# z by DMA transpose and VectorE, tile 0's transposes together, another order of x and W1, and two tiles joined one k step earlier

## The chip, the cores and the metric

The kernel runs on one core of a Trainium2 chip. The metric is the device time of a run in microseconds (us); the median of several runs is given. A profiled run also gives the span, from the first to the last instruction, which is some 2 us shorter here than the run's time.

A core has five engines with an instruction queue each, which run in order and wait for each other by semaphores: TensorE (PE; its weight loads are listed as PEld), VectorE (DVE), ScalarE (ACT), GpSimd (POOL) and SyncE (SP), which only issues DMAs here. Matmuls write into PSUM, which has eight banks of 512 fp32 columns on 128 partitions.

## The reference

The input x has 2048 tokens of 640 features. It is normalized, and the result goes through a linear attention of 32 heads of 20 features and through a GELU MLP with 1536 hidden features. The three terms are added:

```python
xn = _layernorm(x, axis=-1)
return x + _A_ref(xn, A_wqkv, A_wo) + _B_ref(xn, B_w1, B_b1, B_w2, B_b2)

# _A_ref, for each head
phi = lambda t: jnp.where(t > 0, t + 1, jnp.exp(t)) + 1e-6
pq, pk = phi(q), phi(k)
kv = jnp.einsum("bhsd,bhse->bhde", pk, v)
z = jnp.einsum("bhsd->bhd", pk)              # sum of phi(k) over all tokens
num = jnp.einsum("bhqd,bhde->bhqe", pq, kv)
den = jnp.einsum("bhqd,bhd->bhq", pq, z)[..., None] + 1e-6
o = num / den                                # then o @ wo

# _B_ref
h = _gelu(x @ w1 + b1)
return h @ w2 + b2
```

So z holds one number for each of the 640 columns of phi(k): its sum over the 2048 tokens.

## The kernel before

Tokens lie in 16 tiles of 128 (NT = 16, P = 128, DT = 640 / 128 = 5, JT = 1536 / 128 = 12). A planner gives each instruction its waits from what it reads and writes. Within an engine the order is that of the program text.

The stages: (1) x and W1 are loaded, tiles are normalized on VectorE and transposed, and h = gelu(xn @ W1 + b1) is made, with W1's 128x128 blocks as weights and the transposed tokens as moving columns; (2) k and phi(k); (3) G = xn^T phi(k), from which k^T v follows later; (4) q and phi(q), with z and KVT in between; (5) the outputs.

**Loads.** All of these are issued by SyncE, in this order:

```python
for i, (lo, hi) in enumerate(((0, XA), (XA, D))):
    dma(("sync", s_)[i], x_in[:, 0, lo:hi], xv[0:P, lo:hi], [r_x[0][i]])   # second part: ScalarE
dma_x(1, 1)
dma_w1(0)
dma_w1(1)
dma_w1(2)
dma_x(2, 1)
dma_w1(3)
dma_x(3, 1)
dma_w1(4)
dma_x(4, 2)
dma_x(6, 2)
dma_x(8, 2)
dma_x(10, 2)
```

dma_x(t, n) loads tiles t to t+n-1 (160 KB each), dma_w1(k) rows 128k to 128k+127 of W1 (384 KB).

**Tiles 0 to 2** are transposed on TensorE, into banks 6 and 7, and copied from there; tiles 3 to 15 by a DMA transpose that SyncE issues (xnT_dma). PARTS says for a part of tile 0 or 1: bank, first and last 128-column block, copying engine.

```python
PARTS = [((6, 0, 1, s_), (7, 1, 3, s_), (6, 3, DT, s_)), ((6, 0, 3, s_), (7, 3, DT, v))]
# tr_part(t, i): the transposes of part i on TensorE (L342)
# cp_part(t, i): its copy to xnT by ScalarE (L350) or VectorE (L351)
...
tr_part(0, 0)
cp_part(0, 0)
b1_copy()
filler(2, P)
tr_part(0, 1)
cp_part(0, 1)
```

**h of tiles 0 and 1** is built up k step by k step, as W1's row blocks come in, in banks 0 to 5 (hk, L439): one matmul for a block of 128 hidden features, an n of 1 or 2 tiles (128 or 256 moving columns) and one k. Later tiles take whole k sums (h_pack L423, h_unit L408).

```python
plan = k_list(0, 1, [0]) + ["T1"] + k_list(0, 1, [1]) + k_list(1, 1, [0]) + k_list(1, 1, [1]) + ["TC"]
plan += k_list(0, 1, [2]) + k_list(1, 1, [2]) + k_list(0, 2, [3], 0, 8) + ["T2"]
plan += k_list(0, 2, [4], 0, 8) + k_list(0, 2, [3, 4], 8)
plan += pack(2, 0, 8) + h_list(2, 2, 8, JT) + pack(3, 0, 8) + h_list(4, 2, 0, 7) + h_list(6, 2, 0, 7)
plan += h_list(4, 4, 7, JT) + h_list(8, 4, 0, JT) + h_list(12, 4, 0, JT)

def ln_rest():
    def out(t):
        ln_norm(t)
        xnT_dma(t)
    ln_stats(5); out(4); ln_stats(6); out(5)
    ln_stats(7); out(6); out(7)
    dma_x(12, 4)
    ln_stats(8)
    ...                                   # tiles 8 to 15 in the same way

if u == "TC":
    tr_part(0, 2); cp_part(0, 2)
elif u == "T1":
    for i in range(2):
        tr_part(1, i); cp_part(1, i)
    ln_stats(2); ln_half(3, 0); ln_half(3, 1); ln_norm(2); ln_aggr(3)
elif u == "T2":
    at(7)
    b = transp(2)
    ln_norm(3); xnT_dma(3)
    xnT_copy(2, b)
    ln_stats(4); ln_rest()
```

ln_stats is the statistics of a tile (two halves and their aggregate), ln_norm its normalization, all on VectorE with a small step on GpSimd; transp and xnT_copy are tile 2's transposes and copy.

**z.** During stage 3 VectorE adds phi(k) of the 16 tiles (z_sums, L617 and L620), which leaves 128 partial sums for each of the 640 columns, and splits them into a bf16 value and a bf16 remainder (zhl, two times 640 columns, L623 and L626). z_step adds the 128 partitions by a matmul with a column of ones, and spreads z into ZB, the weights of the denominator's matmuls:

```python
def z_step():
    b = take(1)
    Pl.ins(pe, [(lambda e, j=j, i=i: e.matmul(bank(b, j, j + 1), zhl[:, i, j * P:(j + 1) * P], onesm[:, 0:1],
                                              start=(i == 0), stop=(i == 1)))       # L632
                for j in range(DT) for i in range(2)],
           reads=[r_zhl, r_ones], writes=[B_[b]])
    Pl.ins(v, lambda e: e.tensor_copy(z_sb[:], bank(b, 0, DT)), reads=[B_[b]], writes=[r_z])   # L636
    for j in range(DT):
        Pl.ins(v, lambda e, j=j: e.tensor_scalar(ZB[:, j, :], hmask[:, j // 2, :], z_sb[:, j:j + 1], None, ALU.mult),
               reads=[r_z, r_hmask], writes=[r_ZB])                                  # L638

z_sums()
for f in range(DT):
    g_group(f)          # stage 3, L597
g_rem()                 # L606; its result is transposed by DMA, as GrT
...
q_chunk(0)              # q of tiles 0-3: 5 x 5 matmuls L650, phi: ScalarE L552, VectorE L553 and L555
z_step()
kvt_step()              # L660; VectorE masks (L667)
q_chunk(1)
q_chunk(2)
q_chunk(3)
...
out_mm(0, 0, JT, MAIN, first[:1])   # 12 matmuls of output tile 0
den_mm(bb[1])                       # denominators: reads ZB and all of phi(q), head block by head block (L714)
m_step(...)                         # L704
```

The phi instructions on VectorE (0.29 us for L553 and 0.69 us for L555) are issued in each q_chunk, one pair for each of its five banks.

Of the kernel before, what the change touches and what calls it, by code (L numbers as in the profile page):

```python
# [5 lines left out]
ALU = AluOpType  # L6
ACT = mybir.ActivationFunctionType
P = 128
# [104 lines left out]
def bass_parallel_sum__linear_attn_block__dense_activation_gelu__prompt_kernel(  # L113
# [27 lines left out]
    with contextlib.ExitStack() as es:  # L141
# [23 lines left out]
        zsum = Mf[:, 0:2 * D].bitcast(FP32)  # L165
        PKT = Mf[:, 0:NC * CW]
        GrT = Mf[:, 4 * D:5 * D]
        zhl = Mf[:, 2 * D:4 * D].rearrange("p (a d) -> p a d", a=2)
        b1tmp = sb("b1tmp", [JT, P], BF16)
        b1c = sb("b1c", [P, JT], FP32)  # L170
# [8 lines left out]
        aggr = sb("aggr", [P, 4, 2], FP32)  # L179
        rstd = sb("rstd", [P, NT], FP32)  # L180
        mhalf = sb("mhalf", [P, 1], FP32)
        z_sb = sb("z_sb", [P, DT], FP32)
        ek = sb("ek", [P, 3, D], BF16)
        den_sb = sb("den_sb", [P, CW], FP32)
# [55 lines left out]
        r_KVP = [R_("KVP%d" % i) for i in range(3)]  # L240
        r_WqP = R_("WqP")
        r_M = [[R_("M%d_%d" % (j, h)) for h in range(2)] for j in range(DT)]
        r_zsum, r_zhl, r_z, r_ZB = R_("zsum"), R_("zhl"), R_("z"), R_("ZB")
        r_den, r_rden = R_("den"), R_("rden")
        r_rsp = [[R_("rsp%d_%d" % (c, r)) for r in range(3)] for c in range(NC)]
        r_out = [R_("out0"), R_("out1")]
# [18 lines left out]
        def dma_x(t, n):  # L265
            dma("sync", x_in[:, t:t + n, :], xv[t * P:(t + n) * P, :].rearrange("(t p) d -> p t d", p=P),
                sum(r_x[t:t + n], []))

        def dma_w1(k):
            dma("sync", W1[:, k, :], w1v[:, k, :], [r_W1[k]])  # L270
# [3 lines left out]
            dma(("sync", s_)[i], x_in[:, 0, lo:hi], xv[0:P, lo:hi], [r_x[0][i]])  # L274
        dma_x(1, 1)
        dma_w1(0)
        dma_w1(1)
        dma_w1(2)
        dma_x(2, 1)
        dma_w1(3)  # L280
        dma_x(3, 1)
        dma_w1(4)
        dma_x(4, 2)
        dma_x(6, 2)
        dma_x(8, 2)
        dma_x(10, 2)

        Pl.ins(v, lambda e: e.memset(pm[0:P // 2], 1.0), writes=[r_pm])
        Pl.ins(v, lambda e: e.memset(pm[P // 2:P], -1.0), writes=[r_pm])
# [41 lines left out]
        def b1_copy():  # L331
            Pl.ins(s_, lambda e: e.activation(b1c[:], b1T, ACT.Copy), reads=[B_[6]], writes=[r_b1c])

        PARTS = [((6, 0, 1, s_), (7, 1, 3, s_), (6, 3, DT, s_)), ((6, 0, 3, s_), (7, 3, DT, v))]

        def xT(t, k):
            return r_xnT[t][next(i for i, (_, lo, hi, _) in enumerate(PARTS[t]) if lo <= k < hi)]
# [1 line left out]
        def tr_part(t, i):  # L339
            b, lo, hi, _ = PARTS[t][i]  # L340
            pT = bank(b).bitcast(BF16)
            Pl.ins(pe, [(lambda e, k=k: e.transpose(  # L342
                pT[:, k * P:(k + 1) * P], xn_tm[:, t, k * P:(k + 1) * P], ident[:]))
                for k in range(lo, hi)], reads=[r_xn[t][min(i, len(r_xn[t]) - 1)], r_ident], writes=[B_[b]])

        def cp_part(t, i):
            b, lo, hi, eng = PARTS[t][i]
            tok = slice(t * P, (t + 1) * P)
            src = bank(b).bitcast(BF16)[:, lo * P:hi * P].rearrange("p (k q) -> p k q", q=P)
            Pl.ins(eng, lambda e: e.activation(xnT[:, lo:hi, tok], src, ACT.Copy) if eng == s_ else  # L350
                   e.tensor_copy(xnT[:, lo:hi, tok], src), reads=[B_[b]], writes=[r_xnT[t][i]])  # L351

        def ln_half(t, h):
            s = t % 4
            cut = XA if t == 0 else HW
            lo, hi = ((0, cut), (cut, D))[h]
            Pl.ins(v, lambda e: e.bn_stats(stats[:, s, 6 * h:6 * h + 6], x_in[:, t, lo:hi]),  # L357
                   reads=[r_x[t][min(h, len(r_x[t]) - 1)]], writes=[r_stats[s][h]])
            if h == 0:
                Pl.ins(g, lambda e: e.tensor_single_scalar(stats[:, s, 2:3], stats[:, s, 2:3], D * EPS, ALU.add),  # L360
                       reads=[r_stats[s][0]], writes=[r_stats[s][0]])
# [8 lines left out]
        def ln_stats(t):  # L370
            ln_half(t, 0)
            ln_half(t, 1)
            ln_aggr(t)

        def ln_norm(t, part=None):
            s = t % 4
            for i, r in enumerate(r_xn[t]):
                if part not in (None, i):
                    continue
                lo, hi = (0, D) if len(r_xn[t]) == 1 else ((0, P), (P, D))[i]  # L380
                Pl.ins(v, lambda e, lo=lo, hi=hi: e.tensor_scalar(
                    xn_tm[:, t, lo:hi], x_in[:, t, lo:hi], aggr[:, s, 0:1], rstd[:, t:t + 1],
                    ALU.subtract, ALU.mult),
                    reads=r_x[t] + [r_aggr[s], r_rstd[t]], writes=[r])
# [86 lines left out]
        b1_copy()  # L471
        filler(2, P)
        tr_part(0, 1)
        cp_part(0, 1)

        h_list = lambda t, n, lo, hi: [(t, n, jb) for jb in range(lo, hi)]
        k_list = lambda t, n, ks, lo=0, hi=JT: [(t, n, jb, ks) for jb in range(lo, hi)]
        pack = lambda t, lo, hi: [(t, jb) for jb in range(lo, hi, 4)]
        plan = k_list(0, 1, [0]) + ["T1"] + k_list(0, 1, [1]) + k_list(1, 1, [0]) + k_list(1, 1, [1]) + ["TC"]
        plan += k_list(0, 1, [2]) + k_list(1, 1, [2]) + k_list(0, 2, [3], 0, 8) + ["T2"]  # L480
        plan += k_list(0, 2, [4], 0, 8) + k_list(0, 2, [3, 4], 8)
        plan += pack(2, 0, 8) + h_list(2, 2, 8, JT) + pack(3, 0, 8) + h_list(4, 2, 0, 7) + h_list(6, 2, 0, 7)
        plan += h_list(4, 4, 7, JT) + h_list(8, 4, 0, JT) + h_list(12, 4, 0, JT)
# [1 line left out]
# [4 lines that stand above are left out]
            ln_stats(5)  # L489
            out(4)  # L490
            ln_stats(6)
            out(5)
            ln_stats(7)
            out(6)
            out(7)
            dma_x(12, 4)
            ln_stats(8)
            for t in range(8, NT):
                if t + 1 < NT:
                    ln_stats(t + 1)  # L500
                out(t)

        for u in plan:
            if u == "TC":
                tr_part(0, 2)
                cp_part(0, 2)
            elif u == "T1":
                for i in range(2):
                    tr_part(1, i)
                    cp_part(1, i)  # L510
                ln_stats(2)
                ln_half(3, 0)
                ln_half(3, 1)
                ln_norm(2)
                ln_aggr(3)
            elif u == "T2":
                at(7)
                b = transp(2)
                ln_norm(3)
                xnT_dma(3)  # L520
                xnT_copy(2, b)
                ln_stats(4)
                ln_rest()
            elif len(u) == 2:
                h_pack(*u)
            elif len(u) == 4:
                hk(*u)
            else:
                h_unit(*u)
# [98 lines left out]
                       reads=[r_zsum, r_zhl], writes=[r_zhl])  # L628

        def z_step():  # L630
            b = take(1)
            Pl.ins(pe, [(lambda e, j=j, i=i: e.matmul(bank(b, j, j + 1), zhl[:, i, j * P:(j + 1) * P], onesm[:, 0:1],  # L632
                                                      start=(i == 0), stop=(i == 1)))
                        for j in range(DT) for i in range(2)],
                   reads=[r_zhl, r_ones], writes=[B_[b]])
            Pl.ins(v, lambda e: e.tensor_copy(z_sb[:], bank(b, 0, DT)), reads=[B_[b]], writes=[r_z])  # L636
            for j in range(DT):
                Pl.ins(v, lambda e, j=j: e.tensor_scalar(ZB[:, j, :], hmask[:, j // 2, :], z_sb[:, j:j + 1], None, ALU.mult),  # L638
                       reads=[r_z, r_hmask], writes=[r_ZB])

        z_sums()
        for f in range(DT):
            g_group(f)
        g_rem()
# [103 lines left out]
                   reads=[r_xr[t // CH], r_b2], writes=[r_xb[t]])  # L748

        q_chunk(0)  # L750
        z_step()
        kvt_step()
        q_chunk(1)
        q_chunk(2)
# [139 lines left out]
```

## Time and profile before

| | before |
|---|---|
| time, median of 3 | 206.3 us (206.2 to 206.43) |
| span of the profiled run | 204.5 us |
| VectorE busy | 107.6 us (53%) |
| ScalarE busy | 70.6 us (35%) |
| DMA queue of SyncE and that of ScalarE | 32.7% and 6.4% of 16 DMA engines' span |
| moved by DMA | 21.37 MB, mean 105 GB/s |

A line of a timeline has its start and its length in us, the engine, the line of the kernel (L632), the operation, what it writes and reads, the shapes and how many instructions are merged in it; in square brackets stands how long the engine was idle before it, and what ended that. "SPq" is SyncE's queue: for it, the length is that of issuing, not of the transfer. A line of DMA issues ends with the median time from issue to landing. The chain of waits is followed back from the last instruction: at each step to what released it, or to the instruction before it on its engine.

### The profile page before, as it was taken

To read this page: it belongs to the slowest core of one execution; us is meant where nothing else is said; L and a number is where in the kernel's file an instruction comes from. 1 tells how busy PE (TensorE), PEld (TensorE's weight loads), DVE (VectorE), ACT (ScalarE), POOL (GpSimd) and SP (SyncE) were. 2 spreads that over 40 slices of the span, in tenths; PEclk is the share of its full clock that TensorE was granted. 3 is DMA by queue.
4 is the path that set the end of the run, shared out by engine and by line. 5 is a ranking of instruction groups with operands and counts; after the bars stand their busy time and mean duration, and the time that the engine had idled before them with its cause. 6 is when DMAs were issued, how large, how long until landed. Compare 5 with 4: busy or idle time off the path is not lost.

```text
span 204.5 us, 3338 instructions
## 1 busy us (share of the span) xinstructions
PE 201.2 (98%) x1230; PEld 104.0 (51%) x1230; DVE 107.6 (53%) x237; ACT 70.6 (35%) x138; POOL 34.1 (17%) x85
## 2 busy tenths in 40 slices
PE   8999999999999999999999999999999999999995
PEld 3899864444444444444546444544444444444443
DVE  3588764000007889499658888534624823513231
ACT  2369976666676555121163554500000000000000
POOL 3235637400000001898000200000000000000000
PEclk9999999999999999999999999999999999999999
DMA  5997678899700111100010000238985622102301
GB/s 161 368 277 93 136 162 99 233 332 363 250 6 0 26 26 26 29 0 0 0 32 5 0 0 16 92 51 197 321 206 127 152 54 55 51 26 51 79 29 51
DMA packets 34457, 21.37 MB, mean 105 GB/s; under 512 B 21384, under 2 KB 33800, under 8 KB 34440
## 3 DMA queue, kind: packets, MB, share of 16 engines
q1 hardware_dynamic: 30384, 17.54, 32.7%
q10 hardware_dynamic: 4056, 3.61, 6.4%
q8 instruction: 10, 0.16, 0.3%
q14 instruction: 7, 0.06, 0.1%
HBM read 13.08 MB, written 2.62 MB: 77 GB/s over the span
## 4 chain that ended last, share of the span: by engine, by line
PE 96%; DVE 1%; DMA 1%; issue 0%; DVEq 0%
PE ps L771 29%; PE ps L408 20%; PE ps L650 11%; PE ps L564 8%; PE ps L597 8%; PE ps L782 7%; PE ps L439 3%; PE ps L423 2%; PE ps L606 2%; PE ps L570 2%; DMA xPK<-in_A_x_dram 1%; DVE stats L357 1%; PE ps L704 1%; PE ps L660 1%; PE ps L714 1%; PE ps L342 0%
## 5 line engine op out<-in xcount | busy, mean ns | idle before, releaser
L771 PE MATMUL ps<-W,HG 128*128 128x512 bf16 (+2 forms) x204 | 43.9, 367 | 0.0
L408 PE MATMUL ps<-xnT,W 128*128 128x512 bf16 (+1 forms) x235 | 41.5, 338 | 0.0
L412 ACT ACTIVATE HG<-ps,b1c 128x512 bf16<-128x512 f32 (+1 forms) x47 | 27.9, 651 | 12.1 <-PE ps L408 11.6
L408 PEld LDWEIGHTS ps<-xnT,W 128*128 128x128 bf16 x235 | 22.8, 98 | 18.0
L771 PEld LDWEIGHTS ps<-W,HG 128*128 128x128 bf16 x204 | 19.4, 98 | 22.2 <-ACT Msb L686 0.2
L552 ACT ACTIVATE ek<-ps 128x512 bf16<-128x512 f32 x40 | 23.8, 597 | 19.4 <-PE ps L650 10.1
L553 DVE TENSOR_SCALAR ek<-ek 128x512 bf16<-128x512 bf16 x40 | 11.5, 287 | 31.4 <-ACT ek L552 31.4
L795 DVE TENSOR_TENSOR W<-ps,xnT 128x512 bf16<-128x512 f32 x15 | 10.4, 691 | 25.1 <-PE ps L771 19.4
L650 PE MATMUL ps<-xnT,Wqkv 128*128 128x512 bf16 x100 | 21.9, 379 | 0.0
L771 PE MATMUL ps<-Msb,PQ 128*128 128x512 bf16 (+2 forms) x85 | 19.6, 367 | 0.0
L564 PE MATMUL ps<-Wqkv,xnT 128*128 128x512 bf16 x80 | 17.9, 379 | 0.0
L591 POOL COPY Wqkv<-Wqkv 128x128 bf16<-128x128 bf16 x25 | 13.9, 558 | 22.4 <-PE ps L570 20.9
L597 PE MATMUL ps<-xPK,xn_tm 128*128 128x512 bf16 x80 | 17.4, 379 | 0.0
L357 DVE BATCH_NORM_STATS2 stats<-xPK 128x6 f32<-128x320 bf16 (+2 forms) x32 | 13.9, 478 | 5.7 <-DMA xPK<-in_A_x_dram 5.7
L650 PEld LDWEIGHTS ps<-xnT,Wqkv 128*128 128x128 bf16 x100 | 9.7, 98 | 11.5
L555 DVE SCALAR_TENSOR_TENSOR PQ<-ps,ek 128x512 bf16<-128x512 f32 x20 | 13.8, 692 | 2.5 <-PE ps L632 0.5
L771 PEld LDWEIGHTS ps<-Msb,PQ 128*128 128x128 bf16 x85 | 8.2, 98 | 9.2
L597 PEld LDWEIGHTS ps<-xPK,xn_tm 128*128 128x128 bf16 x80 | 7.8, 98 | 9.4
L564 PEld LDWEIGHTS ps<-Wqkv,xnT 128*128 128x128 bf16 x80 | 7.8, 98 | 9.4
L555 DVE SCALAR_TENSOR_TENSOR xPK<-ps,ek 128x512 bf16<-128x512 f32 x16 | 11.1, 692 | 1.7
L620 DVE TENSOR_TENSOR Msb<-Msb,xPK 128x640 f32<-128x640 f32 x14 | 11.6, 826 | 0.5
L367 POOL TENSOR_TENSOR rstd<-aggr,mhalf 128x1 f32<-128x1 f32 x16 | 10.0, 623 | 7.4 <-DVE aggr L365 7.4
(79 smaller groups left out, 151.1 us busy)
## 6 DMA issues: line engine op xcount, KB each, us to landing
Wqkv<-in_A_wqkv_dram SPq DMA_DIRECT2D x3, 800.0 KB, 7.4
xnT<-in_A_x_dram SPq DMA_DIRECT2D x4, 512.0 KB, 6.9
W<-in_B_w_dram SPq DMA_DIRECT2D x5, 384.0 KB, 5.2
W<-in_B_w_dram SPq DMA_DIRECT2D x1, 1920.0 KB, 13.1
out_dram<-W ACTq DMA_DIRECT2D x15, 128.0 KB, 1.8
xn_tm<-rden ACTq DMA_DIRECT2D x12, 128.0 KB, 4.6
xPK<-in_A_x_dram SPq DMA_DIRECT2D x4, 320.0 KB, 7.1
Wo<-in_A_wo_dram SPq DMA_DIRECT2D x8, 160.0 KB, 8.7
```

The source lines that it names most:

```text
L357: Pl.ins(v, lambda e: e.bn_stats(stats[:, s, 6 * h:6 * h + 6], x_in[:, t, lo:hi]), reads=[r_x[t][min(h, len(r_x[t]) - 1)]], writes=[r_stat ...
L408: Pl.ins(pe, [(lambda e, k=k: e.matmul(bank(b, 0, w), W1[:, k, jb * P:(jb + 1) * P], xnT[:, k, tok], start=(k == 0), stop=(k == DT - 1))) ...
L412: Pl.ins(s_, lambda e: e.activation(HG[:, jb, tok], bank(b, 0, w), ACT.Gelu_apprx_tanh, bias=b1c[:, jb:jb + 1]), reads=[B_[b], r_b1c], wri ...
L552: Pl.ins(s_, lambda e: e.activation(e2, src, ACT.Exp), reads=br, writes=[r_ek[s]])
L555: Pl.ins(v, lambda e: e.scalar_tensor_tensor(out=d2, in0=src, scalar=0.0, in1=e2, op0=ALU.max, op1=ALU.add), reads=br + [r_ek[s]], writes= ...
L564: Pl.ins(pe, [(lambda e, k=k, b=b, t=t: e.matmul(bank(b), xnT[:, k, t * P:(t + 1) * P], Wqkv[:, k, D:D + MW], start=(k == 0), stop=(k == D ...
L591: Pl.ins(g, lambda e, k=k, i=i: e.tensor_copy(plain(Wqkv[:, k, D:2 * D], i), parts(Wqkv[:, k, 0:D], i)), reads=[r_Wq], writes=[r_Wk, r_WqP])
L597: Pl.ins(pe, lambda e, t=t, b=b, f=f, i=i: e.matmul(bank(b), xn_tm[:, t, f * P:(f + 1) * P], PK[:, t, 0:MW], start=(i == 0), stop=(i == NT ...
L620: Pl.ins(v, lambda e, t=t: e.tensor_tensor(out=zsum, in0=zsum, in1=PK[:, t, :], op=ALU.add), reads=[r_PK[t], r_PKr[t // CH], r_zsum], writ ...
L650: Pl.ins(pe, [(lambda e, k=k, j=j, b=b: e.matmul(bank(b), Wqkv[:, k, D + j * P:D + (j + 1) * P], xnT[:, k, cc], start=(k == 0), stop=(k == ...
L771: Pl.ins(pe, [(lambda e, i=i, x=x, bk=bk: e.matmul(bank(bk, 0, x[1] - x[0]), seq[i][0], seq[i][1][:, x[0]:x[1]], start=(i == 0), stop=(i = ...
L782: Pl.ins(pe, lambda e, i=i: e.matmul(bank(b), seq[i][0], seq[i][1], start=(i == 0), stop=(i == NS - 1)), reads=seq[i][2], writes=[B_[b]], ...
```

## The change

The change has five parts.

1. z's sum over partitions leaves TensorE: the two times 640 columns of zhl are transposed by DMA (ten blocks of 128x128), VectorE adds along the row and adds value and remainder. This is issued right after z_sums, so it stands before q's phi in VectorE's order. The PSUM bank of the old step is no longer taken.
2. The third part of tile 0's transposes goes into bank 7 and is done right after the second.
3. Tiles 0 and 1 are joined (256 moving columns) from k step 2 on, by counting from 0, instead of from k step 3.
4. Loads: x2 and x3 come between W1's row blocks 0, 1 and 2; x8 to x11 are issued behind tile 5's DMA transpose.
5. Statistics, copies and normalizations of tiles 1 to 3 are reordered on VectorE, and tile 3's normalization and DMA transpose come before tile 2's transposes are used.

```diff
+        zT = Mf[:, 0:2 * D].rearrange("p (a q) -> p a q", q=P)
...
+        z2 = sb("z2", [P, 2 * DT], FP32)
...
         dma_x(1, 1)
         dma_w1(0)
+        dma_x(2, 1)
         dma_w1(1)
+        dma_x(3, 1)
         dma_w1(2)
-        dma_x(2, 1)
         dma_w1(3)
-        dma_x(3, 1)
         dma_w1(4)
         dma_x(4, 2)
         dma_x(6, 2)
-        dma_x(8, 2)
-        dma_x(10, 2)
...
-        PARTS = [((6, 0, 1, s_), (7, 1, 3, s_), (6, 3, DT, s_)), ((6, 0, 3, s_), (7, 3, DT, v))]
+        PARTS = [((6, 0, 1, s_), (7, 1, 3, s_), (7, 3, DT, s_)), ((6, 0, 3, s_), (7, 3, DT, v))]
...
         tr_part(0, 1)
+        tr_part(0, 2)
         cp_part(0, 1)
+        cp_part(0, 2)
...
-        plan = k_list(0, 1, [0]) + ["T1"] + k_list(0, 1, [1]) + k_list(1, 1, [0]) + k_list(1, 1, [1]) + ["TC"]
-        plan += k_list(0, 1, [2]) + k_list(1, 1, [2]) + k_list(0, 2, [3], 0, 8) + ["T2"]
+        plan = k_list(0, 1, [0]) + ["T1"] + k_list(0, 1, [1]) + k_list(1, 1, [0]) + k_list(1, 1, [1])
+        plan += k_list(0, 2, [2]) + k_list(0, 2, [3], 0, 8) + ["T2"]
...
             out(4)
             ln_stats(6)
             out(5)
+            dma_x(8, 2)
+            dma_x(10, 2)
             ln_stats(7)
...
-            if u == "TC":
-                tr_part(0, 2)
-                cp_part(0, 2)
-            elif u == "T1":
-                for i in range(2):
-                    tr_part(1, i)
-                    cp_part(1, i)
+            if u == "T1":
+                tr_part(1, 0)
+                cp_part(1, 0)
+                tr_part(1, 1)
                 ln_stats(2)
                 ln_half(3, 0)
+                cp_part(1, 1)
+                ln_norm(2)
                 ln_half(3, 1)
-                ln_norm(2)
                 ln_aggr(3)
+                ln_norm(3)
+                xnT_dma(3)
             elif u == "T2":
                 at(7)
                 b = transp(2)
-                ln_norm(3)
-                xnT_dma(3)
                 xnT_copy(2, b)
...
         def z_step():
-            b = take(1)
-            Pl.ins(pe, [(lambda e, j=j, i=i: e.matmul(bank(b, j, j + 1), zhl[:, i, j * P:(j + 1) * P], onesm[:, 0:1],
-                                                      start=(i == 0), stop=(i == 1)))
-                        for j in range(DT) for i in range(2)],
-                   reads=[r_zhl, r_ones], writes=[B_[b]])
-            Pl.ins(v, lambda e: e.tensor_copy(z_sb[:], bank(b, 0, DT)), reads=[B_[b]], writes=[r_z])
+            dma_t("sync", zT, Mf[:, 2 * D:4 * D], [r_zT, r_zsum], reads=[r_zhl])
+            Pl.ins(v, lambda e: e.tensor_reduce(out=z2[:], in_=zT, axis=mybir.AxisListType.X, op=ALU.add), reads=[r_zT], writes=[r_z2])
+            Pl.ins(v, lambda e: e.tensor_tensor(out=z_sb[:], in0=z2[:, 0:DT], in1=z2[:, DT:2 * DT], op=ALU.add),
+                   reads=[r_z2], writes=[r_z])
...
         z_sums()
+        z_step()
...
         q_chunk(0)
-        z_step()
         kvt_step()
```

More of the change, by code (lines that the diff above doesn't have):

```diff
@@ L242, in bass_parallel_sum__linear_attn_block__dense_activation_gelu__prompt_kernel @@
         r_M = [[R_("M%d_%d" % (j, h)) for h in range(2)] for j in range(DT)]
-        r_zsum, r_zhl, r_z, r_ZB = R_("zsum"), R_("zhl"), R_("z"), R_("ZB")
+        r_zT, r_z2, r_zsum, r_zhl, r_z, r_ZB = R_("zT"), R_("z2"), R_("zsum"), R_("zhl"), R_("z"), R_("ZB")
         r_den, r_rden = R_("den"), R_("rden")
```

## The prediction

> **What bounds the kernel now.** I read four views in this order: busy time per engine, the chain of waits (first its shares, then in order of time), the timelines of the three stages that the diff touches, and the DMA issues one at a time.
>
> The page says that the span is TensorE:
>
> ```profile
> PE 201.2 (98%) x1230; PEld 104.0 (51%) x1230; DVE 107.6 (53%) x237; ACT 70.6 (35%) x138; POOL 34.1 (17%) x85
> ...
> PE 96%; DVE 1%; DMA 1%; issue 0%; DVEq 0%
> ```
>
> The first line is busy time, the second the share of each engine in the chain that ended last. The chain in order of time (start, length, what; all in us) shows the start of the kernel and the place of z's matmuls:
>
> ```profile
> 5.83 0.28 PE ps L342 x2
> 6.11 0.01 issue
> 6.12 0.83 PE ps L439 x12
> 6.95 0.31 PE ps L342 x5
> 7.26 2.01 PE ps L439 x36
> 9.28 0.11 PE ps L342 x2
> 9.39 2.21 PE ps L439 x32
> 11.60 0.28 PE ps L389 x5
> ...
> 107.94 0.23 PE ps L632 x10
> ```
>
> From 6.12 us on there is no other engine in the chain until the last VectorE instruction. A busy TensorE may still hide short waits, because a matmul's end is modelled, so I go by starts. Five transposes in a row take 0.28 us (56 ns each), the 215 matmuls from 20.41 us take 38.94 us, and I get 109 ns for a start to the next one at 256 columns and 216 ns at 512. Against those spacings I looked for larger ones and found two that the change can touch. One is before 6.12: two transposes start at 5.83 and 5.89, the first W1 matmul only at 6.12. The other is here (weight loads, one merged row per run):
>
> ```profile
> 15.25 0.43 PEld L423 LDWEIGHTS ps<-xnT,W 128*128 128x128 bf16 x7
> 15.82 0.22 PEld L408 LDWEIGHTS ps<-xnT,W 128*128 128x128 bf16 x3
> ```
>
> The first run ends at 15.68, the next begins at 15.82: 0.13 us in which TensorE waits. L408 is the first group that needs tile 3, and tile 3 comes by the first of these DMA transposes, whose own time to landing is the second line:
>
> ```profile
> 12.63 9.09 SPq L263 DMA_TRANSPOSE xnT<-xn_tm  x5
> ...
> xnT<-xn_tm SPq DMA_TRANSPOSE x1, 3.1
> ```
>
> 12.63 + 3.15 = 15.78, just before 15.82. For z I need VectorE's order around it:
>
> ```profile
> 99.45 1.60 DVE L626 TENSOR_TENSOR Msb<-Msb 128x128 bf16<-128x128 f32 x5
> 104.29 0.29 DVE L553 TENSOR_SCALAR ek<-ek 128x512 bf16<-128x512 bf16 x1 [3.25 <-ACT ek L552]
> ...
> 109.89 0.15 DVE L636 COPY z_sb<-ps 128x5 f32<-128x5 f32 x1
> 110.08 1.31 DVE L638 TENSOR_SCALAR ZB<-hmask,z_sb 128x32 bf16<-128x32 bf16 x5
> 111.31 1.27 DVE L667 TENSOR_TENSOR W<-ps,maskKV 128x320 bf16<-128x320 f32 x3
> ...
> 126.88 0.69 DVE L555 SCALAR_TENSOR_TENSOR PQ<-ps,ek 128x512 bf16<-128x512 f32 x1
> ```
>
> The parts of zsum are ready at 101.05, VectorE then idles 3.25 us, and the last phi of q ends at 127.57.
>
> **What the Trainium skill says.** "TensorE: Matmul & The Clock Gate", section "Wait — 56ns, not 53.3ns?", gives a spacing of N / 2.4 GHz plus about 2.5 ns on the warm clock; the trace's 56, 109 and 216 ns agree. So joining two 128-column matmuls saves only that fixed part. "VectorE: DVE Perf Modes", section "The perf-mode tier table (the rule you actually need)", says that tensor_reduce runs at 1x whatever its type; no tensor_reduce is in this trace. "DMA: Bandwidth & Descriptors", section "Queues, rings and completion order", says that each DMA engine takes the descriptors of a ring in ring order; so what SyncE issues first is fetched first. The trace agrees: the five W1 blocks and x tiles land in their order of issue.
>
> **The change part by part.**
>
> *z.* Ten one-column matmuls leave TensorE: 0.23 us by the chain (ten spacings of 25 ns). On the path: -0.23. They are replaced by a DMA transpose of 1280 columns, a reduce of 128x1280 and an add, and ZB's five instructions now stand ahead of q's phi on VectorE. A transpose of 512 to 640 columns takes 2.4 to 2.6 us with the queue empty (2.4 for the PK ones, 2.6 for GrT), and its packets move in well under 1 us, so I estimate 3.0 to 3.4 us for 1280 columns: landing near 104.3. The reduce at 1x, estimated from the 128x640 fp32 add of 826 ns (page; 640 more elements at about 1.04 ns) is near 1.5 us, the add about 0.15, ZB 1.31: done near 107.3. The first phi then starts at 107.3 instead of 104.29. Five phi at 1.0 us each (108.90 to 109.89 in the trace) end at 112.3, the mask multiply of KVT at 113.5, against 112.5 before. Fifteen phi of 0.99 us follow: end near 128.4, against 127.57. The only reader with a deadline is the denominator matmul of the last head block: it starts 128.41 + 0.10 + 4 x 0.216 = 129.4 before, some 0.4 us earlier now, 129.0. Banks: a bank comes back after eight groups, 8.6 us; VectorE's lag stays under 5. So it is hidden, by about 0.6 us.
>
> *k step 2 joined.* 24 spacings of 55.7 ns (1.34 us) become 12 of 109 (1.31): -0.03.
>
> *Tile 0's transposes together.* The last two now run right behind the first two, between 5.95 and 6.06, in the hole before 6.12, instead of taking 0.11 us at 9.28: -0.11.
>
> *What it costs.* All of parts 1 and 2 of tile 0 now sit in bank 7, where tile 1's second part also goes, so that part waits until ScalarE has copied both. Four transposes end near 6.22, the first copy runs 6.26 to 6.64, the second to about 6.98; with some 0.12 us from ScalarE's end to TensorE's start (5.98 to 6.12 in the trace) tile 1's second part starts at 7.10 instead of 6.98, and k step 1 at 7.22 instead of 7.10. W1's block 1 lands at 6.72 before and now has x2 ahead of it (160 KB, about 0.45 us): 7.15 to 7.2. Both waits run in parallel and end together: +0.13. Block 2 has x2 and x3 ahead, 7.83 + 0.9 = 8.7, needed at 9.26: free. Sum of the start so far: -0.11 - 0.03 + 0.13, about zero.
>
> *x2, x3 earlier.* VectorE waits for x2 until 8.36 and for x3 until 10.05. Now both have landed by 7.7; tile 3's normalization ends near 10.7 instead of 12.61, and its transpose, issued some 1.9 us earlier, lands near 14, long before 15.7. The wait of 0.13 goes: -0.13.
>
> *x8 to x11 later.* They leave the queue when W1, x4 and x6 are being fetched and come back behind tile 5's transpose, near 17.6 us. Needed by VectorE for tile 8, which then is done 1 to 2 us later than at 19.23; tiles 8 to 11 are first used on TensorE near 33.4 and their last transpose landed at 31.2, after x12's landing at 27.0, which hardly moves. Hidden. The close one is tiles 6 and 7, whose transposes now queue behind 640 KB of x: tile 7's landed at 19.61 + 3.57 = 23.2, and TensorE comes to it at 20.25 + 35 x 0.109 = 24.07. I put its landing at 23 to 24: on average +0.05.
>
> Sum: -0.23 - 0.03 - 0.11 + 0.13 - 0.13 + 0.05 = -0.32, and a little of the 0.13 may not come: 206.3 - 0.35 = 205.95 us.
>
> **The rivals.** *VectorE takes over in the q stage.* For it: it is busy 14.45 of the 16.2 us from 109.6 to 125.8, so it can win back hardly anything, and z's DMA now stands in its line. If the transpose of 1280 columns takes 5 us, the last phi ends at 130 and TensorE waits 1 us: 206.9. Against it: 3.25 us of idle stand just where the transpose runs, and ZB leaves its old place (1.5 us). *The later x load starves tiles 6 and 7.* For it: one queue, a margin of 0.9 us, and two of the old transposes there already took 3.9 and 3.6 us instead of 2.6. It would cost 0.2 to 1 us: 206.2 to 206.9. Against it: VectorE's earlier start on tile 4 (by about 0.5 us) makes room. *W1 comes too late at the start.* Blocks 1 and 2 give up their lead of 0.4 and 1.4 us; a slower fetch shows at once on TensorE, up to 0.3 us: 206.2. *Everything hidden but z:* 206.07.
>
> **Range and chances.** The removable part is known within 0.1: at best 0.23 + 0.03 + 0.11 + 0.13 = 0.50, so 205.8, and 205.6 with the scatter of single times (0.1 to 0.2). The three rivals cost upward of that, mostly under 0.6. I predict 205.95, range 205.6 to 206.5. 2% is 4.1 us, far outside all of this: faster 0.01, same 0.98, slower 0.01.
>
> **What would show it.** In the changed profile: no L632 in the chain; the weight-load hole at 15.7 gone, as tile 3's transpose is issued near 10.7; transposes from 5.83 unbroken to the first W1 matmul at 6.1; a new hole of about 0.1 near 7.1; VectorE's first phi of q near 107 and its last ending near 128; no hole near 24 or in the denominator matmuls. I am wrong if z's transpose takes over 4 us, if TensorE waits near 24 us, or if W1's blocks 1 or 2 hold it for over 0.3 us.

## The result and the profile after

The changed kernel takes 207.47 us (median of 6 runs, 207.14 to 207.98) against 206.31: a ratio of 1.0058, 95% interval 1.0043 to 1.0073. It is slower by 1.2 us, within 2%, and outside the range of 205.6 to 206.5. The profiled run has a span of 205.5 us against 204.5.

The page of the changed kernel, busy time and the shares of the chain:

```profile
PE 200.2 (97%) x1191; PEld 103.6 (50%) x1208; DVE 109.0 (53%) x238; ACT 70.5 (34%) x138; POOL 34.1 (17%) x85
...
PE 88%; DMA 5%; DVE 2%; issue 1%; SPq 1%; ACT 1%; POOL 1%; DVEq 0%
```

TensorE's share of the chain fell from 96% to 88%: DMAs now release it. Which ones, the chain in order of time says (start, length, what):

```profile
2.67 4.91 DMA W<-in_B_w_dram
7.58 0.05 issue
7.62 4.37 PE ps L439 x56
...
19.13 0.01 issue
19.14 5.51 DMA xnT<-xn_tm
24.65 0.68 issue
25.32 3.98 PE ps L408 x35
```

Two waits are new: one that ends at 7.62 with a block of W1 (issued at 2.67: block 1), and one that ends at 25.32, at the 35 matmuls of tiles 6 and 7. The chain follows tile 6's transpose, landed at 24.65; the 0.68 us of "issue" behind it are tile 7's, as the matmuls need both. (The pieces of 0.05 us that the chain has at regular distances later on are matmul records that are missing; the starts around them are two matmuls apart.) The weight loads show both waits in square brackets, and that the old one is gone:

```profile
7.62 0.34 PEld L439 LDWEIGHTS ps<-xnT,W 128*128 128x128 bf16 x6 [0.47 <-DMA W<-in_B_w_dram]
...
14.92 1.16 PEld L423 LDWEIGHTS ps<-xnT,W 128*128 128x128 bf16 x20
16.03 0.48 PEld L408 LDWEIGHTS ps<-xnT,W 128*128 128x128 bf16 x5
...
23.89 0.32 PEld L408 LDWEIGHTS ps<-xnT,W 128*128 128x128 bf16 x3
25.30 0.34 PEld L408 LDWEIGHTS ps<-xnT,W 128*128 128x128 bf16 x4 [1.09 <-DMA xnT<-xn_tm]
```

The second and third rows follow each other without a hole: tile 3 no longer keeps TensorE waiting at 15.7. Before the change the weight load that now starts at 25.30 (the 56th of its line) started at 23.96, with nothing in square brackets:

```profile
23.96 0.42 PEld L408 LDWEIGHTS ps<-xnT,W 128*128 128x128 bf16 x4
```

The DMA issues of tiles 6 and 7, asked one at a time (last column: us to landing), were issued at 19.14 and 20.40:

```profile
xnT<-xn_tm SPq DMA_TRANSPOSE x1, 5.5
...
xnT<-xn_tm SPq DMA_TRANSPOSE x1, 4.8
```

Before the change they were issued at 18.37 and 19.61:

```profile
xnT<-xn_tm SPq DMA_TRANSPOSE x1, 3.9
...
xnT<-xn_tm SPq DMA_TRANSPOSE x1, 3.6
```

So tile 7 landed at 25.2 instead of 23.2. And VectorE's order around z:

```profile
105.69 1.49 DVE L634 TENSOR_REDUCE z<-Msb 128x10 f32<-128x1280 bf16 x1 [3.39 <-DMA Msb<-Msb]
107.21 0.17 DVE L635 TENSOR_TENSOR z_sb<-z 128x5 f32<-128x5 f32 x1
107.41 1.31 DVE L638 TENSOR_SCALAR ZB<-hmask,z_sb 128x32 bf16<-128x32 bf16 x5
108.63 0.29 DVE L555 TENSOR_SCALAR ek<-ek 128x512 bf16<-128x512 bf16 x1
...
129.12 0.69 DVE L557 SCALAR_TENSOR_TENSOR PQ<-ps,ek 128x512 bf16<-128x512 f32 x1
```

The idle time of 3.25 us before the first phi has become the wait for z's transpose (3.39), and q's first phi starts right behind ZB, at 108.63 instead of 104.29. VectorE is late there and TensorE is not: the denominators still follow the matmul before them with the same spacing as before the change (309 ns in both traces).

**Where the time went.** The weight load for the first matmul of tile 6 starts at 23.96 us before and at 25.30 after: +1.34. From there to the end it is 180.50 us before and 180.17 after: -0.33, of which z is 0.25 (from the first q matmul to the first KVT matmul 5.65 us before, 5.40 after); the rest is that a weight load runs further ahead of its matmul when nothing is waited for. Together that is +1.01 us, the difference of the two spans; the medians of the times differ by 1.16. The change won what it was to win in z, and lost more ahead of tile 6, 1.0 us of it in the wait at that point.

### The profile page after: what moved, and what is told of

The parts are those of the page before. It is cut to its first block, busy times and chain, and to the rows that moved or that the text cites. A ratio compares the mean times of both kernels' runs of the same rounds, so it can differ in the third digit from the quotient of the medians.

```text
span 205.5 us, 3272 instructions
## 1 busy us (share of the span) xinstructions
PE 200.2 (97%) x1191; PEld 103.6 (50%) x1208; DVE 109.0 (53%) x238; ACT 70.5 (34%) x138; POOL 34.1 (17%) x85
## 4 chain that ended last, share of the span: by engine, by line
PE 88%; DMA 5%; DVE 2%; issue 1%; SPq 1%; ACT 1%; POOL 1%; DVEq 0%
PE ps L771 28%; PE ps L408 17%; PE ps L651 10%; PE ps L599 8%; PE ps L566 8%; PE ps L782 7%; DMA xnT<-xn_tm 3%; DMA W<-in_B_w_dram 2%; PE ps L439 2%; PE ps L572 2%; PE ps L608 2%; DVE stats L357 1%; SPq L262 1%; ACT Msb L687 1%; PE ps L661 1%
## 5 line engine op out<-in xcount | busy, mean ns | idle before, releaser
L408 PEld LDWEIGHTS ps<-xnT,W 128*128 128x128 bf16 x235 | 22.8, 98 | 18.9 <-DMA xnT<-xn_tm 1.1
L771 PEld LDWEIGHTS ps<-W,HG 128*128 128x128 bf16 x204 | 19.5, 98 | 22.2 <-ACT Msb L687 0.2
L795 DVE TENSOR_TENSOR W<-ps,xnT 128x512 bf16<-128x512 f32 x15 | 10.4, 691 | 24.5 <-PE ps L771 19.4
L771 PE MATMUL ps<-Msb,PQ 128*128 128x512 bf16 (+2 forms) x84 | 19.5, 366 | 0.1
L557 DVE SCALAR_TENSOR_TENSOR xPK<-ps,ek 128x512 bf16<-128x512 f32 x16 | 11.1, 692 | 1.7
```

What stands on the lines that cost most here:

```text
L408: Pl.ins(pe, [(lambda e, k=k: e.matmul(bank(b, 0, w), W1[:, k, jb * P:(jb + 1) * P], xnT[:, k, tok], start=(k == 0), stop=(k == DT - 1))) ...
L557: Pl.ins(v, lambda e: e.scalar_tensor_tensor(out=d2, in0=src, scalar=0.0, in1=e2, op0=ALU.max, op1=ALU.add), reads=br + [r_ek[s]], writes= ...
L771: Pl.ins(pe, [(lambda e, i=i, x=x, bk=bk: e.matmul(bank(bk, 0, x[1] - x[0]), seq[i][0], seq[i][1][:, x[0]:x[1]], start=(i == 0), stop=(i = ...
```

## The experiments

Each group of runs stands beside runs of the kernel before on the same chip, which took 206.5 to 206.7 us there; so the ratio is what is compared. "Tile 6" is the start of the first weight load that needs tiles 6 and 7, "wait" is what TensorE lost there beyond its normal spacing, by the starts of its matmuls, and "rest" is from there to the end of the span. These three are of one profiled execution each; those of e7 and e14 took 208.19 and 208.07 us, some 1 us more than the medians of their kernels (207.08 and 207.12), so the losses that they show are likely larger than those of most runs.

| run | ratio (95%) | tile 6, us | wait, us | rest, us |
|---|---|---|---|---|
| before | 1 | 23.96 | 0 | 180.50 |
| changed | 1.0058 (1.0043 to 1.0073) | 25.30 | 1.00 | 180.17 |
| changed, second time (e13) | 1.0026 (1.0015 to 1.0036) | 24.95 | 0.56 | 180.18 |
| e1: x8 to x11 back | 1.0001 (0.9988 to 1.0014) | 24.61 | 0 | 180.25 |
| e2: W1, x2, x3 back | 1.0051 (1.0031 to 1.0071) | 25.34 | 1.19 | 180.18 |
| e3: both back | 0.9990 (0.9978 to 1.0001) | 24.43 | 0 | 180.26 |
| e4: z alone | 0.9990 (0.9976 to 1.0003) | 24.16 | 0 | 180.25 |
| e6: x8 to x11 behind tile 3 | 0.9978 (0.9970 to 0.9987) | 24.51 | 0 | 180.26 |
| e7: x8 to x11 behind tile 7 | 1.0031 (1.0010 to 1.0051) | 24.88 | 0 | 181.59 |
| e8: half of x8 to x11 back | 0.9996 (0.9983 to 1.0008) | 24.69 | 0.58 | 180.19 |
| e9: x8 to x11 from ScalarE | 1.0075 (1.0057 to 1.0093) | 26.60 | 0 | 180.25 |
| e10: 12 more matmuls | 1.0041 (1.0023 to 1.0058) | 25.31 | 1.13 | 180.18 |
| e11: e6 and W1 in another order | 0.9963 (0.9949 to 0.9976) | 23.70 | 0 | 180.26 |
| e12: e11 with the old z | 0.9979 (0.9966 to 0.9992) | 23.70 | 0 | 180.51 |
| e14: 40 more matmuls | 1.0027 (1.0013 to 1.0041) | 26.16 | 1.17 | 180.18 |
| e15: e11 and 40 more | 1.0028 (1.0017 to 1.0038) | 25.54 | 0 | 180.27 |
| e16: e2 and the copy first | 1.0035 (1.0023 to 1.0048) | 25.75 | 1.47 | 180.18 |

**Theory A** was that the two new orders of loads cost the time, x8 to x11 at 24 us and x2, x3 at 7 us; **its rivals** that z's new way costs it, or chance in the fetching of W1, or an instruction fetch.

### e1: x8 to x11 back in their old place

```diff
         dma_x(6, 2)
+        dma_x(8, 2)
+        dma_x(10, 2)
...
             out(5)
-            dma_x(8, 2)
-            dma_x(10, 2)
```

> The changed kernel with the loads of x8 to x11 back in their old place, behind x6. Theory A (x8 to x11 ahead of the transposes of tiles 6 and 7 in SyncE's queue hold them up): the hole of 1.0 us at 24 us goes; tile 3's transpose now queues behind x8 to x11 and lands near 15.5, so up to 0.1 us may come back near 15.7; time about 206.5 us. Rival B (the 1.0 us comes from something else at that point, such as an instruction fetch on the same DMA engines, or from z): the hole stays at 0.7 us or more and the time is within 0.3 us of 207.4.

The wait at 24 us is gone. Tile 3's transpose, as foreseen, went behind x8 to x11, but it landed at 16.4 and not at 15.5, and its wait came back larger than before the change:

```profile
15.44 0.60 PEld L425 LDWEIGHTS ps<-xnT,W 128*128 128x128 bf16 x10
16.47 0.55 PEld L410 LDWEIGHTS ps<-xnT,W 128*128 128x128 bf16 x6 [0.43 <-DMA xnT<-xn_tm]
```

Still the ratio falls from 1.0058 (or 1.0026) to 1.0001. Theory A stands for x8 to x11.

### e2: the old order of W1 and x2, x3

```diff
         dma_w1(0)
-        dma_x(2, 1)
         dma_w1(1)
-        dma_x(3, 1)
         dma_w1(2)
+        dma_x(2, 1)
         dma_w1(3)
+        dma_x(3, 1)
         dma_w1(4)
```

> The changed kernel with the old order of W1 and x2, x3. Theory A (x2 ahead of W1's block 1 costs the hole of 0.46 us at 7.1): that hole goes, and what stays is the wait at 24 us; time about 207.0 us. Rival (W1's first blocks were merely fetched more slowly in the profiled run): the hole stays between 0.2 and 0.5 us, time about 207.4. Tile 3's transpose then goes out near 12.4, and 0.1 us may come back near 15.7.

The wait for W1 went in this profile (a wait of 0.14 us for bank 7 took its place, and 0.09 us came in near 10.7). That the order alone did it is not shown: W1's block 0, which x2 does not stand ahead of, landed at 5.39 here and at 6.16 in the changed kernel. In e3 and e16, with this same old order, it landed at 6.58 and 6.31 and TensorE waited; in e8, with the changed order, it landed at 5.64 and there was no wait for W1. And the time did not fall: what TensorE won ahead of tile 6 it waited there, 1.19 us.

### e3: both back

> Both orders of loads back, so z by DMA transpose, tile 0's transposes together, the earlier joining and VectorE's new order alone. Theory A: no hole at 7.1 nor at 24; 206.3 less 0.23 (z), 0.03 (joining), 0.11 (transposes): about 205.95, or 206.05 with the wait for tile 3. Rival (z's DMA and VectorE's lag cost time that the holes hide): 206.3 or more.

0.9990: no wait at 24 us, and a gain on the kernel before of some 0.2 us that its interval (0.9978 to 1.0001) just fails to show. The trace shows two reasons why it is not more. W1's block 0 landed late in this execution, at 6.58, and the first matmul of h started at 6.63 instead of 6.12:

```profile
6.63 0.56 PE L441 MATMUL ps<-xnT,W 128*128 128x128 bf16 x7 [0.48 <-DMA W<-in_B_w_dram]
```

And late x2 and x3 hold up VectorE, while the change had put tile 1's copy behind the first half of tile 3's statistics in its order. VectorE's timeline, with TensorE waiting 0.23 us for that copy at 11.1:

```profile
10.33 0.50 DVE L359 BATCH_NORM_STATS2 stats<-xPK 128x6 f32<-128x320 bf16 x1 [0.22 <-DMA xPK<-in_A_x_dram]
10.74 0.28 DVE L353 COPY xnT<-ps 128x256 bf16<-128x256 bf16 x1
```

### e4: z alone

The kernel before, with z by DMA transpose and VectorE, issued right after the sums.

> The kernel before with z by DMA transpose and VectorE alone. If z's matmuls were on the path and what takes their place is hidden: 0.23 us less than before, 206.08 us, and no hole in the denominator matmuls near 128. If VectorE becomes the bound of the q stage: 206.5 or more, with a hole of 0.3 us or more there.

0.9990 (0.9976 to 1.0003): the interval holds the predicted 0.9989 and also 1. The trace decides it: from the first q matmul to the first KVT matmul 5.40 us instead of 5.65, the rest 180.25 instead of 180.50, and no wait at the denominators. z is worth its 0.25 us.

### e6: x8 to x11 right behind tile 3's transpose

```diff
                 ln_norm(3)
                 xnT_dma(3)
+                dma_x(8, 2)
+                dma_x(10, 2)
...
             out(5)
-            dma_x(8, 2)
-            dma_x(10, 2)
```

> The changed kernel with x8 to x11 issued right behind tile 3's transpose, so behind it but ahead of those of tiles 4 to 7, in a stretch in which SyncE's queue stood empty (14.4 to 16.5 us). If only the place in the queue matters: no wait at 24 us (tile 7 lands near 23.2, as before the change) and no wait for tile 3 (its transpose is first, landing near 14.4); what stays is W1's block 1 near 7.1; time about 206.3, some 1.1 us under the changed kernel. Rival (any load of x8 to x11 after tile 3 runs into the transposes): tile 4's or 5's transposes land late and a hole of 0.5 us or more stands between 20 and 24 us.

0.9978: the place counts. x8 to x11 land at 16.3 and 17.2, the transposes of tiles 4 to 6 take 2.6 us each, no wait at 16 nor at 24 us. Tile 7 landed at 23.9, later than expected, with TensorE there at 24.5.

### e7: x8 to x11 behind tile 7's transpose

> The changed kernel with x8 to x11 still later, behind tile 7's transpose. Theory A: tiles 6 and 7 no longer queue behind them, the hole at 24 us goes; tile 8's statistics start 2 us later again and tiles 8 to 11 land near 33 to 34.5, which is just about when TensorE comes to them (33.4), so a new hole of 0 to 1 us near 33 instead. Time 206.3 to 207.3. Rival (an instruction fetch on the same DMA engines alone delays tiles 6 and 7): the hole at 24 us stays at 0.5 us or more.

Both halves came: no wait at 24 us, and a new one for tiles 8 to 11, of 1.33 us by the starts of the matmuls. (The first half had help: W1's block 2 landed at 10.25 and held TensorE for 0.63 us, so that it came to tile 6 late, at 24.88, with tile 7 landed at 24.33.)

```profile
32.91 0.96 PEld L408 LDWEIGHTS ps<-xnT,W 128*128 128x128 bf16 x5
35.50 0.56 PEld L408 LDWEIGHTS ps<-xnT,W 128*128 128x128 bf16 x4 [1.63 <-issue]
```

Tile 6's transpose, with no copy ahead, took 2.6 us here, tile 7's 4.3. A transpose lands in sixteen parts. For tile 7 fifteen of them had landed after 2.7 us; the last came 1.5 us later.

### e8: half of it

> The changed kernel with only x8 and x9 (320 KB) behind tile 5's transpose, x10 and x11 back behind x6. Theory A in the form 'what counts is the bytes ahead in the queue': 320 KB less are 0.85 us, tile 7 lands near 24.3 instead of 25.2, the hole at 24 us shrinks from 1.0 to about 0.2 us; tile 3's transpose lands near 15.3, in time; time about 206.6. Rival (a fixed delay of some 2 us, from an instruction fetch that holds one DMA engine, whatever the bytes): the hole stays near 1.0 us, time 207.4.

Here x10 and x11 went back behind x6, and x8 and x9 stayed behind tile 5's transpose. The wait was 0.58 us, between the two expectations. Tile 7 landed at 24.63: against the two profiles of the changed kernel (25.23, and 24.89 in e13) half the bytes took away 0.3 to 0.6 us and not 0.85. Tile 6's transpose took 5.6 us with half the bytes ahead, as long as with all of them. Bytes are one part of the cause, not the whole.

### e9: x8 to x11 from ScalarE's queue

```diff
+            elif u == "X8":        # in the plan behind the packs of tile 2
+                for t in (8, 10):
+                    dma(s_, x_in[:, t:t + 2, :], ...)
```

> The changed kernel with x8 to x11 issued from ScalarE's queue, near 18.5 us, so at the same time but in another ring of the same DMA engines. If the ring's order is what holds tiles 6 and 7 up: their transposes land at 22 to 23.3 as before the change, no hole at 24 us, time about 206.4 (ScalarE loses 1 us to issuing, which the free banks cover). If the sharing of the DMA engines is what counts: tile 7 lands at 24 us or later, and a hole of 0.3 us or more stays; time about 207.

Another queue does not help. The copies were issued at 16.80 and 17.24, the transpose of tile 5 at 17.26, and it took 5.5 us, with no instruction fetch near; TensorE lost 1.88 us there instead. So a transpose beside copies is held up even when they come from another queue, and the order within one ring can't be the whole cause. (The prediction cited the ring's order from the Trainium skill, "DMA: Bandwidth & Descriptors", section "Queues, rings and completion order". It may still count in the changed kernel: in the six runs in which SyncE issued x10 just ahead of tile 6's transpose, tile 6 landed 0.58 to 0.63 us behind x10 each time, at 24.65 and 24.05 in the changed kernel. No run tells the two apart.)

### e13: the changed kernel once more

> The changed kernel itself once more, on the same chip as these: a ratio to the kernel before of 1.004 to 1.007, the wait for W1's block 1 at 7.1 us (0.2 to 0.5 us) and the wait for tile 7 at 24 us (0.7 to 1.3 us). If the two waits were chance of one profile: less than half of that.

1.0026, less than expected, and the same two waits, 0.36 and 0.56 us: not chance of one profile. The second is below the 0.7 to 1.3 us that were expected, though more than half of the first profile's 1.00. That this wait varies fits the two ratios; with one profile each it is not shown to be their cause.

### e10 and e14: TensorE's instruction fetch

In each trace a packet of 16 KB on a queue of kind "instruction" falls between 18 and 26 us. In the DMA view of the changed kernel from 21.5 to 22.5 us:

```profile
q8 instruction: 1, 0.02, 8.3%
```

It began at 21.8 and held one DMA engine for 1.3 us. Before the change it came at 19.5. The Trainium skill, "Runtime: NRT & Kernel Launch", section "Instruction fetch mechanics", says that a sequencer refills its instructions in blocks of 16 KiB (256 instructions) by a DMA queue of its own, mostly hidden. The traces agree with the block: the later fetches come near TensorE's 320th, 447th and 568th matmul (within ten, in every run; a weight load and a matmul are two instructions). For the other work of the DMA engine it is not hidden, as e14 shows. The two runs add matmuls that compute nothing at the start, to move the fetch. The twelve of e10 fit into idle time; the forty of e14 do not, and the first matmul of h started at 6.70 there instead of 6.20, which the wait for W1 then swallowed (k step 1 at 7.65 instead of 7.62).

```diff
-        filler(5, P)
+        filler(17, 40)      # e10; in e14: filler(45, 24)
```

> The changed kernel with twelve more matmuls that compute nothing at the very start (17 of 40 columns instead of 5 of 128), so that TensorE's count of instructions is as before the joining. Theory F: the 16 KB instruction fetch seen at 21.4 to 22.3 us (19.5 before) is TensorE's, comes at a fixed count of its instructions, and holds one DMA engine for over 1 us, so that the DMA transposes of tiles 6 and 7, which need all engines, stand still; with the count restored it comes near 20 us, in the loads of x8 to x11, the hole at 24 us shrinks to 0.5 us or less, time 206.9 or less. Rival Q (only the 640 KB ahead in the queue count): the hole stays at 0.8 to 1.2 us and the time near 207.5.

Twelve more moved the next fetch from 36.0 us (e13) to 33.5, by twelve matmuls of 216 ns, but this one stayed at 21.25, and the wait at 1.13 us. As it stood, theory F fell; but the fetch had not been moved out of the way, so it was not a test of its effect.

> The changed kernel with forty more matmuls that compute nothing at the start (45 of 24 columns instead of 5 of 128). With twelve more, the later instruction fetches came earlier by just twelve matmuls (36 to 33.5 us), but the one near 21.5 us did not move, as if it had waited for its DMA engine. With forty more it should come before the copies of x8 to x11 start, near 16.5 to 18.5 us. Theory F (the late landing of tiles 6 and 7 is the copies and the fetch together): tile 7 lands near 23.3 instead of 24.9 to 25.2, no hole at 24 us, a ratio to the kernel before of 0.997 to 1.000. Rival Q (the copies alone): the hole stays at 0.5 to 1.2 us, a ratio of 1.003 to 1.005.

Forty more moved it to 18.4 us. The expected result did not come: 1.0027, and the wait for tiles 6 and 7 stayed at 1.17. But the trace shows what a fetch does. It now met tile 4's transpose, and the weight loads stood still for tiles 4 and 5:

```profile
19.90 0.60 PEld L423 LDWEIGHTS ps<-xnT,W 128*128 128x128 bf16 x10
21.17 0.67 PEld L408 LDWEIGHTS ps<-xnT,W 128*128 128x128 bf16 x7 [0.67 <-DMA xnT<-xn_tm]
```

Tile 4's transpose took 4.3 us and not 2.6, again with one part that landed 1.9 us behind the first. SyncE, held up in issuing tile 5's, sent x8 to x11 two microseconds later (20.06 instead of 18.00), and so tiles 6 and 7 came late from there. But they came in the same order and at the same distances as in the changed kernel, only without the fetch. SyncE's issues in the changed kernel, and then in e14:

```profile
18.00 1.10 SPq L262 DMA_DIRECT2D xPK<-in_A_x_dram  x2
19.14 2.55 SPq L265 DMA_TRANSPOSE xnT<-xn_tm  x2
...
20.06 1.09 SPq L262 DMA_DIRECT2D xPK<-in_A_x_dram  x2
21.20 2.54 SPq L265 DMA_TRANSPOSE xnT<-xn_tm  x2
```

The second of the two copies, x10, landed 5.4 us after its issue in the changed kernel (4.9 to 5.6 in the five runs of this order with the fetch in that time) and 3.6 us in e14; the transposes of tiles 6 and 7 took 3.7 and 3.6 us in e14, against 5.5 and 4.8:

```profile
xPK<-in_A_x_dram SPq DMA_DIRECT2D x1, 320.0 KB, 5.4
...
xPK<-in_A_x_dram SPq DMA_DIRECT2D x1, 320.0 KB, 3.6
...
xnT<-xn_tm SPq DMA_TRANSPOSE x1, 3.7
...
xnT<-xn_tm SPq DMA_TRANSPOSE x1, 3.6
```

That gives the parts, all from issue to landing:

| what met the transpose | us |
|---|---|
| nothing (e7, tile 6; e6, tile 6) | 2.6 |
| the copies of x8 to x11 (e14, tiles 6 and 7) | 3.6 to 3.7 |
| the fetch (before, tile 6; e6, e7 and e11, tile 7) | 3.9 to 4.4 |
| both (changed, e2, e8, e10, e13 and e16, tile 6) | 5.0 to 5.6 |
| copies from ScalarE's queue, no fetch (e9, tile 5) | 5.5 |

In SyncE's queue the copies add 1.1 us, the fetch 1.3 to 1.8, and the sum, 5.0 to 5.5, is what both together took. The last row shows that this is no general rule: with the copies in the other queue 5.5 us came about without a fetch. That the fetch is what delayed tiles 6 and 7 before the change and in e6, e7 and e11 rests on these traces, in which it falls into the transpose; no run moved it away from them with all else kept.

### e11, e12: a version without the two waits

e6, with x2 and x3 one place later than in the change, and tile 1's copy first again on VectorE:

```diff
         dma_w1(0)
-        dma_x(2, 1)
         dma_w1(1)
-        dma_x(3, 1)
+        dma_x(2, 1)
         dma_w1(2)
+        dma_x(3, 1)
...
                 tr_part(1, 1)
+                cp_part(1, 1)
                 ln_stats(2)
                 ln_half(3, 0)
-                cp_part(1, 1)
```

> x8 to x11 right behind tile 3's transpose (as in the run before that did this), x2 and x3 one place later (behind W1's blocks 1 and 2 instead of 0 and 1), and VectorE's copy for tile 1 back ahead of the statistics of tiles 2 and 3. If x2 and x3 ahead of W1 cost 0.2 to 0.4 us in the run with x8 to x11 behind tile 3: about 205.9, a ratio to the kernel before of 0.996 to 0.997. If W1's blocks are late by themselves: 206.15, a ratio of 0.998.

> The same with z by TensorE's ten one-column matmuls, as before. If z by DMA and VectorE is worth its 0.23 us of TensorE: 0.2 to 0.25 us above the run with the new z. If what took its place costs as much somewhere: no difference, or less.

e11 is faster than both kernels: 0.9963 (0.9949 to 0.9976), 205.98 us against 206.68 on that chip. Its chain, from 6 us on, runs on TensorE without a break to the end of stage 1 (tile 1's transposes fill the stretch from 6.90 to 7.28; the list leaves out short pieces):

```profile
6.17 0.73 PE ps L439 x12
7.28 4.19 PE ps L439 x56
11.75 1.75 PE ps L439 x16
13.50 2.23 PE ps L423 x40
15.73 2.18 PE ps L408 x20
17.91 2.23 PE ps L423 x40
20.15 38.94 PE ps L408 x215
```

The last row is the one that began at 20.41 before the change: 0.26 us earlier. With the old z it is 0.9979, 0.0016 or 0.3 us more, though the two intervals overlap; in the two traces the rest differs by 180.51 - 180.26 = 0.25 us, z again.

### e15, e16: two remainders

> The version with x8 to x11 behind tile 3's transpose and x2, x3 one place later, with the same forty matmuls at the start. No copy stands ahead of tiles 6 and 7 there, yet tile 7's transpose took 4.4 us, with a fetch at 21.0 us. Theory F: with the fetch away it takes 2.6 to 3.0 us and lands near 21.7. Rival Q: it still takes over 4 us. The time is the same either way, within 0.2 us, as TensorE waits for nothing there.

With the fetch at 18.9 us, tile 7's transpose took 3.6 us and not 2.6 to 3.0. Fifteen of its sixteen parts had landed after 2.7 us, with x12 issued right behind it; the last came 0.9 us later. Another instruction fetch, of 8 KB on another queue, lies there; the view is of 23.3 to 24.3 us, and the packet began at 23.4:

```profile
q14 instruction: 1, 0.01, 2.0%
```

That this packet held up the last part is likely and not shown. That TensorE would wait for nothing was wrong: it lost 0.89 us at tiles 4 and 5, whose transposes met the large fetch and took 5.0 and 4.2 us. Nor were the forty matmuls free. They kept TensorE busy beyond the time at which tile 0 could be transposed (5.4 us in e11), and the first matmul of h started at 6.74 instead of 6.06:

```profile
4.64 1.37 PE L321 MATMUL ps<-const-bfloat16-1.0 128*128 128x24 bf16 x45
...
6.74 0.83 PE L439 MATMUL ps<-xnT,W 128*128 128x128 bf16 x12
```

Waits for W1 of 0.24 and 0.17 us came on top. So of what e15 lost against e11 the fetch explains a part only.

> The changed kernel with the old order of W1 and x2, x3, and with VectorE's copy for tile 1 ahead of the statistics of tiles 2 and 3 again, so that late x2 and x3 do not hold it up. What x2 ahead of W1's block 1 costs by itself is the difference to the changed kernel: 0.2 to 0.4 us less, a ratio of 0.0010 to 0.0020 below its 1.0026 to 1.0058, and no wait for W1 at 7.1 us; the wait for tile 7 at 24 us stays, longer by about what the start became shorter. If that longer wait takes it all back: no difference.

No difference to the changed kernel that its interval shows (1.0035 against 1.0026 and 1.0058). In this run TensorE waited 0.29 us for W1 even in the old order, since the first block itself came late, and 1.47 us at tile 6. In the changed kernel the order of W1 is worth next to nothing, as what is won at the start is waited for at 24 us.

## Why the prediction was wrong

**The step that failed** is the one on x8 to x11: "I put its landing at 23 to 24: on average +0.05". Tile 7 landed at 25.2 (24.9 in the second run), and the term was +1.0 (0.56). The rival was named, with its place, its reason and up to 1 us of cost, but I weighed it at a twentieth of that. Two sizes were wrong in it. I named the 3.9 and 3.6 us that two transposes took in the profile of before, with no copy of x ahead of them, and did not ask why: an instruction fetch lies there, at 19.5. So the margin of 0.9 us was measured with one delay already in it, and that of the copies came on top. And I took the transposes of tiles 6 and 7 to be issued about when they were, while SyncE issues x8 and x10 first: 19.14 instead of 18.37. Two of the three signs of being wrong that the prediction names came: TensorE waited near 24 us, and W1's block 1 held it for over 0.3 us. The range failed because two rivals came true at once, with 1.0 and 0.54 us, while it left 0.55 us upward.

**W1's block 1**: predicted +0.13, measured 0.46 at 7.1 us plus 0.08 before 6.2. It landed at 7.58, not at 7.2, mainly because block 0 had come at 6.16 instead of 5.48; it landed between 5.3 and 6.8 us over the runs, with either order of loads, and what makes it vary is open. The wait for bank 7, which I had put beside it, was not seen in the changed kernel; where W1 came in time (e2, e11) it was 0.14 and 0.07 us, against 0.12 predicted.

**z**: right in each part. -0.23 predicted, -0.25 measured; transpose 3.0 to 3.4 us, measured 3.3; reduce 1.5, measured 1.49; add 0.15, measured 0.17; the lag of VectorE hidden. tensor_reduce at 1x, as the Trainium skill has it ("VectorE: DVE Perf Modes", section "The perf-mode tier table (the rule you actually need)"), fits: 1.49 us for 1280 elements.

**Tile 3, the joining, tile 0's transposes**: right. The hole at 15.7 is gone, the four transposes run unbroken from 5.82; what the joining saves was not measured by itself. Together with the two W1 waits they bring TensorE to tile 6 at +0.27 us: 0.46 + 0.08 - 0.13 - 0.11 - 0.03 = 0.27; the trace has 24.22 against 23.96 if the wait there is left out.

**What I had not seen** is that these terms could not add up at all. In the changed kernel the landing of tile 7 is set by VectorE and the DMAs, not by TensorE; any gain of TensorE ahead of it is waited away (e2, e16), and only what comes behind it, z, reaches the end.

## What to carry to other kernels

Before a load is moved ahead of transfers that the bottleneck waits for, take the margin of those transfers from the profile, ask what delays are already in it, and add the time of issuing, the copies' time and the instruction fetches up, as if none hid behind another. Loads that are not urgent fit where the DMA queue stands empty (here behind tile 3's transpose, which cost no wait at 24 us in e6 and e11), and neither another queue (e9) nor a later place (e7) is a cure by itself. When terms of a sum lie on both sides of a new wait, only those behind it count.

## What the runs showed of the hardware that I had not expected

- The packet of a 16 KB instruction fetch, TensorE's by its count, took 0.9 to 1.7 us, and a DMA transpose of 128x640 that met it landed in 3.8 to 4.5 us instead of 2.6, in one part of sixteen or as a whole. In e1, e7 and e14, where one part alone was late, it landed 1.05 to 1.09 us after the end of that packet. The fetch comes near a count of TensorE's instructions, so adding or joining matmuls moves it, and with it which transpose is late.
- With plain copies of 640 KB ahead in the same queue such a transpose took 3.6 to 3.7 us (e14); beside copies from another queue it took 5.5 us (e9).
- The first fetch in this stretch does not follow its count strictly: twelve more matmuls moved the next one by 2.5 us and this one by 0.5 (e10, against e13). That it waits for room on its DMA engine is a guess that no run tested.
